# A second table that fixes the place of some 290 of the first 430 instructions

## The chip, the cores and the metric

The kernel runs on one core of one Trainium2 chip. The metric is the device time of one execution in microseconds (us). The kernel before took 1061.97 us, the median of three runs (1061.06, 1062.64 and 1061.97).

## What is computed

Three layers follow each other, all in float32 with an accuracy that plain single-pass matmuls would not give:

```
attention:  q, k, v of shape (4, 12, 448, 64): batch, heads, tokens, width of a head
            q, k are divided by their root mean square and multiplied by g_q, g_k
            softmax(q k^T / 8) v
layer 1:    x (1792 x 768) @ w_in (768 x 1024) -> h;  h * softmax(h), layer norm times g_ln,
            @ w_out (1024 x 768)
layer 2:    x (1792 x 768) @ w_in (768 x 2048) -> h;  h - tanh(h), @ w_out (2048 x 768)
```

The weights arrive as 64-bit floats and are turned into pairs of 32-bit halves (a high part and the rest) on the chip.

## The kernel before

Attention works on 24 pairs of heads. For each pair p: `load_qk` and `load_v` fetch the data; `norm` squares, sums and scales (tiles sq, ss, nr, rr, qn; on VectorE for the first two pairs, on GpSimd for the others); `qk_trans` transposes on TensorE (qkps) and splits the result into high and low parts (wk, wq), and eight DMAs spread these over the tiles k and q, of which there are three each, used in turn; `maxima` multiplies q by k once in a rough form (mps) and takes the row maximum on VectorE (nm); `spread` transposes the maxima (nmps, nt) and a DMA puts them as an extra row into q; `weights` makes the exact scores (sps), and ScalarE takes their exponential (pf); `pv` multiplies by v (pvps); `pv_fin` and `x_norm` divide and write the result to xd. Tiles mps and sps share three PSUM buffers, pvps has two, and qkps, nmps and the others share three.

Pair 0 is made in another way than the rest: its scores come from four matmuls with a contraction over 64 rows each (rows 0 to 63 for the first head, 64 to 127 for the second), while every later pair has two matmuls over 128 rows. In the profile these are `sps<-q,k 64*128` and `sps<-q,k 128*128`. The transposes (112 rows), pair 1's mps (128 rows) and most of pvps (128 rows) use the whole height of the array.

None of this is issued in the order in which it is written. A recorder takes down some 4,000 operations, `place` plays them through a list scheduler with estimated costs (`cost`) and a table of offsets by tile name (`SHIFT`), and `give` issues them in the order found, on all engines' queues at once. Where the planner expects TensorE to wait, `fill` puts dummy matmuls in front of the instruction that is waited for: 128x128 products of a tile of ones (`idle<-still`), whose number is the expected wait divided by a fixed cost. Each is two passes in the profile. Their number is settled in `place`:

```
n = int((start - since - 0.1) / took)
...
for _ in range(n):
    ...
    order.append(op)
```

Every operation is recorded from one line, L206, so the rows of the profile tell operations apart by their tiles. Each engine executes its own queue strictly in the order issued; SyncE's queue holds nearly all DMA issues. A DMA takes one of eight semaphores in turn, and its issue waits until the one eight places ahead of it has landed. The recorded stretch holds the attention and the beginning of layer 1; the first 430 operations of it are what the change touches.

Of the kernel before, what the change touches and what calls it, by code (L numbers as in the profile page):

```python
# [167 lines left out]
def _real(x):  # L168
# [14 lines left out]
    "wq scalar": -28, "wq vector": -149, "x scalar": -868, "x2d sync": 478, "x2ps tensor": 274, "xd sync": -164,  # L183
    "xo scalar": -435, "xo vector": -40, "xr sync": 224, "xs scalar": -251, "xs vector": 13, "xu scalar": -29,
    "xu vector": -999, "zero vector": 166,
}


class Recorder:
# [307 lines left out]
    slack, doubt = (0.12, 0.39), 0.97  # L497
    still = None

    def give(self):  # L500
        order = self.plan()
        self.on = False
        with self.tc.manual_schedule():
            for op in order:
                self.take(op.queue, op.what, op.f, op.a, op.kw)
        self.ops = []
# [884 lines left out]
```

## Time and profile before

| | us |
|---|---|
| median of three runs | 1061.97 |
| profiled execution, its own time | 1057.57 |
| span of the profiled execution | 1055.5 |
| TensorE busy in the span | 1037.0 (98%) |
| VectorE busy | 686.8 (65%) |
| ScalarE busy | 490.9 (47%) |
| GpSimd busy | 234.8 (22%) |
| granted TensorE clock, mean | 1.00 of full |

The profile is of one execution. Its time is the span and 2.07 us around it. "Busy" TensorE contains the dummy matmuls, and the ends of matmuls are modelled, so the 98% does not mean that useful products fill the span. In the tables by stretch, a row gives for each engine the busy time in the stretch and the count of instructions, then the granted clock, the mean busy share of the 16 DMA engines and what they moved.

### The profile page before, as it was taken

The numbers are of one execution on the slowest core, as the hardware profiler recorded it, in microseconds if no ns is written. First come the engines' busy times: TensorE is split into PE (matmuls) and PEld (weight loads), VectorE is DVE, ScalarE is ACT, GpSimd is POOL, SyncE is SP. The second block draws the span as 40 slices with busy tenths as digits, with TensorE's granted clock in tenths as the row PEclk, the third lists the DMA queues.
The fourth block names the chain that finished last, engine by engine and source line by source line (L and its number), as shares of the span: only waits on it lengthen the run. The fifth ranks groups of instructions, "written<-read, shape, count | busy, mean of one in ns | idle before, by whom it ended". The sixth has DMA issues, their size and how long they took to land.

```text
span 1055.5 us, 15572 instructions
## 1 busy us (share of the span) xinstructions
PE 1037.0 (98%) x5550; PEld 877.5 (83%) x5550; DVE 686.8 (65%) x1312; ACT 490.9 (47%) x996; POOL 234.8 (22%) x204
## 2 busy tenths in 40 slices
PE   9999999999998999999999999999999999999998
PEld 7665686768866788787999999898989999998988
DVE  8877867988898533538731373666768576765434
ACT  5878867898887543742451443212222221212110
POOL 3423132221203100025000251413333241412000
PEclk9999999999999999999999999999999999999999
DMA  7899988998999994676865421212212021110004
GB/s 190 237 243 228 253 256 251 257 250 274 288 301 253 307 291 159 202 251 200 289 215 189 165 71 51 60 60 60 61 40 79 22 61 42 59 60 1 1 30 179
DMA packets 112469, 171.20 MB, mean 162 GB/s; under 512 B 30656, under 2 KB 78216, under 8 KB 112392
## 3 DMA queue, kind: packets, MB, share of 16 engines
q1 hardware_dynamic: 112368, 170.20, 55.0%
q8 instruction: 44, 0.72, 0.3%
q14 instruction: 33, 0.27, 0.1%
q10 hardware_dynamic: 24, 0.01, 0.0%
HBM read 109.32 MB, written 29.10 MB: 131 GB/s over the span
## 4 chain that ended last, share of the span: by engine, by line
PE 81%; DMA 7%; DVE 5%; ACT 3%; issue 1%; SPq 1%; POOL 1%; DVEq 0%; ACTq 0%; POOLq 0%
PE ops L206 22%; PE h2ps L206 22%; PE x2ps L206 9%; PE hps L206 9%; PE pvps L206 8%; PE sps L206 5%; PE mps L206 3%; DMA q<-wq 2%; DMA xr<-xd 1%; DVE val L206 1%; PE qkps L206 1%; DMA q<-nt 1%; SPq L206 1%; DMA raw<-in_moe_w_in_dram 1%; PE idle L206 1%
## 5 line engine op out<-in xcount | busy, mean ns | idle before, releaser
L206 PE MATMUL ops<-w,gT 128*128 128x384 f32 x1344 | 257.5, 336 | 0.0
L206 PE MATMUL h2ps<-x2s,w 128*128 128x512 f32 (+1 forms) x1152 | 256.4, 365 | 0.0
L206 PEld LDWEIGHTS ops<-w,gT 128*128 128x128 f32 x1344 | 235.8, 188 | 8.4
L206 PEld LDWEIGHTS h2ps<-x2s,w 128*128 128x128 f32 x1152 | 200.2, 188 | 27.8
L206 DVE SCALAR_TENSOR_TENSOR val<-raw,val 128x512 int32<-128x512 int32 (+1 forms) x192 | 147.4, 771 | 58.9 <-POOL val L206 56.7
L206 DVE TENSOR_TENSOR ob<-ops,ob 128x384 f32<-128x384 f32 x196 | 108.4, 554 | 102.4 <-PE ops L206 102.0
L206 POOL TENSOR_TENSOR w<-val,w 128x512 fp32r<-128x512 f32 x60 | 80.8, 1348 | 374.0 <-ACT w L206 363.3
L206 PE MATMUL pvps<-pf,va 128*128 128x448 f32 (+1 forms) x384 | 156.5, 555 | 0.0
L206 DVE TENSOR_REDUCE nm<-mps 128x1 f32<-128x448 f32 x168 | 100.0, 618 | 53.0 <-PE mps L206 52.5
L206 PE MATMUL hps<-w,xs 128*128 128x256 f32 (+1 forms) x828 | 126.2, 308 | 2.3 <-ACT hb L206 2.3
L206 PE MATMUL sps<-q,k 128*128 128x448 f32 (+2 forms) x400 | 125.8, 431 | 2.8 <-DMA q<-nt 1.6
L206 PEld LDWEIGHTS hps<-w,xs 128*128 128x128 f32 x828 | 114.5, 190 | 12.0 <-ACT hb L206 3.2
L206 PE MATMUL x2ps<-lnT,w 128*128 128x384 f32 (+1 forms) x720 | 121.4, 326 | 0.3 <-DVE lnT L206 0.3
L206 PEld LDWEIGHTS x2ps<-lnT,w 128*128 128x128 f32 x720 | 116.8, 188 | 3.4 <-issue 2.2
L206 ACT ACTIVATE th<-h2ps 128x512 f32<-128x512 f32 (+1 forms) x64 | 34.8, 544 | 179.3 <-PE h2ps L206 167.0
L206 PEld LDWEIGHTS sps<-q,k 128*128 128x128 f32 (+2 forms) x400 | 67.4, 182 | 44.2 <-issue 22.1
L206 ACT ACTIVATE pf<-sps 128x448 f32<-128x448 f32 (+1 forms) x169 | 87.0, 537 | 21.6 <-PE sps L206 20.3
L206 PEld LDWEIGHTS pvps<-pf,va 128*128 128x128 f32 (+1 forms) x384 | 60.2, 188 | 36.8 <-issue 33.2
L206 POOL TENSOR_SCALAR val<-raw 128x512 f32<-128x512 f32 x48 | 77.8, 1622 | 32.7 <-DMA raw<-in_moe_w_out_dram 13.2
L206 ACT ACTIVATE gT<-th 128x512 fp32r<-128x512 f32 (+1 forms) x64 | 37.1, 579 | 99.4 <-PE ops L206 66.8
L206 POOL TENSOR_TENSOR qn<-qk,rr 112x512 f32<-112x512 f32 x44 | 50.4, 1165 | 114.7 <-issue 30.9
L206 DVE TENSOR_TENSOR th<-h2ps,th 128x512 f32<-128x512 f32 (+1 forms) x64 | 39.8, 621 | 43.8 <-ACT th L206 43.7
(95 smaller groups left out, 990.2 us busy)
## 6 DMA issues: line engine op xcount, KB each, us to landing
w<-w_out SPq DMA_DIRECT2D x48, 512.0 KB
raw<-in_moe_w_in_dram SPq DMA_DIRECT2D x36, 512.0 KB
raw<-in_moe_w_out_dram SPq DMA_DIRECT2D x36, 512.0 KB
w<-w_in SPq DMA_DIRECT2D x24, 512.0 KB
k<-wk SPq DMA_DIRECT2D x46, 224.0 KB
q<-wq SPq DMA_DIRECT2D x46, 224.0 KB
w_in<-w SPq DMA_DIRECT2D x12, 512.0 KB
w_out<-w SPq DMA_DIRECT2D x12, 512.0 KB
```

The lines of the kernel that those rows point to most:

```text
L206: return f(*[_real(x) for x in a], **{n: _real(x) for n, x in kw.items()})
```

## The change

A table `PLACE` maps the number of an operation (the sequence in which it was recorded) to a position. `placed` first cuts the planned order into groups: an operation with the dummy matmuls that stand ahead of it. Groups named in the table go to the positions given there; the others fill the positions that are left, in their planned sequence. The table has 287 entries with positions up to 428; from position 429 on nothing is moved. The planner itself, its costs and the number of dummy matmuls are as before: the dummies travel with the instruction that they stand ahead of.

```diff
+PLACE = {
+    3: 0, 4: 3, 266: 4, 157: 5, 158: 6, 81: 7, 7: 9, 83: 10, 6: 11, 82: 12, 261: 13, 160: 14, 0: 15, 79: 16, 8: 19,
...
+}
...
+    def placed(self, order):
+        still, groups = [], []
+        for op in order:
+            still.append(op)
+            if op.at >= 0:
+                groups.append(still)
+                still = []
+        rest = iter([g for g in groups if g[-1].at not in PLACE])
+        held = {PLACE[g[-1].at]: g for g in groups if g[-1].at in PLACE}
+        return [op for n in range(len(groups)) for op in (held[n] if n in held else next(rest))] + still
+
     def give(self):
-        order = self.plan()
+        order = self.placed(self.plan())
```

Three places show what moves. In these rows k_182 and q_167 are pair 0's k and q before, k_156 and q_164 the same tiles after; k_163 and q_177 (before), k_161 and q_166 (after) belong to pair 1.

GpSimd's first instructions, before:

```order
L1372 MEMSET const-uint8-127 128x1
L1386 UNCONDITIONAL_BRANCH
masks.py:197 MEMSET idf 128x128
L206 MEMSET va 128x7x64 x2
masks.py:199 ISA
masks.py:199 AFFINE_SELECT idf<-idf 128x128
L206 CAST q_167<-zero 64x448 x2
L206 CAST q_177<-zero 64x448 x2
L206 CAST q_185<-zero 64x448 x2
```

And after:

```order
L1412 MEMSET const-uint8-127 128x1
L1426 UNCONDITIONAL_BRANCH
masks.py:197 MEMSET idf 128x128
masks.py:199 ISA
masks.py:199 AFFINE_SELECT idf<-idf 128x128
L235 CAST q_164<-zero 64x448
L235 CAST q_166<-zero 64x448
L235 CAST q_164<-zero 64x448
L235 CAST q_166<-zero 64x448
L235 MEMSET va 128x7x64
```

Two memsets of v's tiles leave the place ahead of the identity matrix idf and come far later.

TensorE around the longest row of dummies, before:

```order
L206 MATMUL mps<-k_182,q_167 128x448
L206 MATMUL nmps<-idf,nm 4x128
L206 MATMUL mps<-wk,qd_155 128x448
L206 MATMUL idle<-still 128x128 x4
L206 MATMUL nmps<-idf,nm 4x128
L206 MATMUL idle<-still 128x128 x18
L206 MATMUL mps<-k_163,q_177 128x448
L206 MATMUL sps<-q_167,k_182 128x448 x3
L206 MATMUL sps<-q_167,k_163 128x448
L206 MATMUL sps<-q_167,k_182 128x448 x3
```

And after:

```order
L235 MATMUL mps<-k_156,q_164 128x448
L235 MATMUL sps<-q_164,k_156 128x448
L235 MATMUL idle<-still 128x128 x4
L235 MATMUL nmps<-idf,nm 4x128
L235 MATMUL sps<-q_164,k_156 128x448 x2
L235 MATMUL nmps<-idf,nm 4x128
L235 MATMUL sps<-q_164,k_156 128x448
L235 MATMUL mps<-wk,qd_150 128x448
L235 MATMUL idle<-still 128x128 x18
L235 MATMUL mps<-k_161,q_166 128x448
L235 MATMUL sps<-q_164,k_161 128x448
L235 MATMUL sps<-q_164,k_156 128x448
```

Five sps matmuls of pair 0 have come ahead of the 18 dummies, which are as many as before: three of them, with one nmps and one mps, between the nmps that waits for the last maximum and the dummies, one ahead of that nmps, and one further ahead (not shown).

TensorE behind the dummies, where the rest of pair 0's scores is made, before:

```order
L206 MATMUL mps<-k_163,q_177 128x448
L206 MATMUL sps<-q_167,k_163 128x448
L206 MATMUL qkps<-idf,qn 128x112
L206 MATMUL mps<-k_163,q_177 128x448
L206 MATMUL qkps<-idf,qn 128x112 x7
L206 MATMUL sps<-q_167,k_182 128x448
L206 MATMUL mps<-k_163,q_177 128x448
L206 MATMUL sps<-q_167,k_182 128x448 x2
L206 MATMUL nmps<-idf,nm 4x128
L206 MATMUL sps<-q_167,k_163 128x448
L206 MATMUL sps<-q_167,k_182 128x448 x3
L206 MATMUL sps<-q_167,k_163 128x448
```

And after:

```order
L235 MATMUL sps<-q_164,k_161 128x448
L235 MATMUL qkps<-idf,qn 128x112
L235 MATMUL sps<-q_164,k_156 128x448
L235 MATMUL qkps<-idf,qn 128x112
L235 MATMUL mps<-k_161,q_166 128x448
L235 MATMUL qkps<-idf,qn 128x112
L235 MATMUL sps<-q_164,k_156 128x448
L235 MATMUL qkps<-idf,qn 128x112
L235 MATMUL sps<-q_164,k_156 128x448 x2
L235 MATMUL mps<-k_161,q_166 128x448
L235 MATMUL sps<-q_164,k_161 128x448
L235 MATMUL mps<-k_161,q_166 128x448
```

Transposes, rough scores and exact scores now alternate one by one. Counted from pair 1's first mps to the first pvps, pair 0's sps stood in 5 unbroken runs before and stand in 12 after. Further on, the two pvps matmuls over 64 rows, which stood side by side, are separated by others.

## Rows read from the trace of the kernel before

**Rows 1.** The page: busy time, share of the span, instructions of each engine.

```profile
PE 1037.0 (98%) x5550; PEld 877.5 (83%) x5550; DVE 686.8 (65%) x1312; ACT 490.9 (47%) x996; POOL 234.8 (22%) x204
```

**Rows 2.** Busy time by stretch: start:end, length, engines, clock, DMA share, GB/s.

```profile
0.00:25.00 25.00, 22.62 (x152) 19.81 (x153) 21.49 (x61) 13.38 (x33) 8.04 (x17) 1.00 0.83 199
25.00:55.00 30.00, 29.58 (x141) 19.50 (x141) 25.17 (x53) 23.73 (x54) 12.39 (x12) 1.00 0.87 228
...
350.00:400.00 50.00, 49.30 (x291) 41.37 (x291) 19.20 (x31) 23.45 (x53) 0.84 (x3) 1.00 1.00 302
```

**Rows 3.** The same view for the dummies alone (PE, PEld, clock, DMA).

```profile
0.00:25.00 25.00, 17.65 (x122) 16.47 (x122) 1.00 0.83 199
25.00:55.00 30.00, 2.20 (x14) 2.18 (x14) 1.00 0.87 228
```

**Rows 4.** Chain that ended last, first 60 us: start, length, what.

```profile
0.86 0.89 POOL va L206 x2
...
21.67 2.81 DMA q<-wq
```

**Rows 5.** TensorE's timeline 18 to 29 us: start, length, instructions [idle before].

```profile
19.87 0.27 PE L206 MATMUL nmps<-idf,nm 128*4 128x128 f32 x1
19.98 4.18 PE L206 MATMUL idle<-still 128*128 128x128 f32 x36
24.47 0.44 PE L206 MATMUL mps<-k,q 128*128 128x448 f32 x1 [0.31 <-DMA q<-wq]
24.85 3.41 PE L206 MATMUL sps<-q,k 64*128 64x448 f32 x19
28.19 0.47 PE L206 MATMUL mps<-k,q 128*128 128x448 f32 x1
28.59 0.47 PE L206 MATMUL sps<-q,k 64*128 64x448 f32 x1
28.99 0.32 PE L206 MATMUL qkps<-idf,qn 112*128 112x112 f32 x1
```

**Rows 6.** The same timeline, 29 to 34 us.

```profile
29.45 0.83 PE L206 MATMUL qkps<-idf,qn 112*128 112x112 f32 x7
30.21 0.47 PE L206 MATMUL sps<-q,k 64*128 64x448 f32 x1
30.61 0.47 PE L206 MATMUL mps<-k,q 128*128 128x448 f32 x1
31.01 0.67 PE L206 MATMUL sps<-q,k 64*128 64x448 f32 x2
...
31.81 1.34 PE L206 MATMUL sps<-q,k 64*128 64x448 f32 x9
33.08 0.47 PE L206 MATMUL mps<-k,q 128*128 128x448 f32 x1
33.88 0.47 PE L206 MATMUL mps<-k,q 128*128 128x448 f32 x1 [0.33 <-ACT pf L206]
```

**Rows 7.** The same timeline, 36 to 47 us.

```profile
36.33 1.67 PE L206 MATMUL pvps<-pf,va 128*128 128x448 f32 x4
37.83 0.55 PE L206 MATMUL qkps<-idf,qn 112*128 112x112 f32 x4
38.31 1.02 PE L206 MATMUL pvps<-pf,va 64*128 64x448 f32 x4
39.27 1.49 PE L206 MATMUL sps<-q,k 128*128 128x448 f32 x6
...
45.62 0.38 PE L206 MATMUL idle<-still 128*128 128x128 f32 x2
46.09 1.09 PE L206 MATMUL sps<-q,k 128*128 128x448 f32 x4
```

**Rows 8.** TensorE's waits, 55 to 500 us: total, times, longest. The costliest.

```profile
PE mps L206 <- ACT pf L206: 3.4, 4, 1.5
```

**Rows 9.** VectorE's timeline: the last row maximum ahead of the 18 dummies.

```profile
18.77 0.62 DVE L206 TENSOR_REDUCE nm<-mps 128x1 f32<-128x448 f32 x1 [0.57 <-PE mps L206]
```

24 rows, old and new, of the table PLACE are left out of this document.

## The prediction

> **What bounds the kernel now.** I read the page first, then the tables by stretch, the chain, and TensorE's timeline around the change. TensorE is busy for 98% of the span [rows 1], at a granted clock of 1.00 in every stretch [rows 2], so the other engines, at 65% and less, can only matter through waits that they cause. But the first stretch is not what it seems: of the 22.6 us that TensorE is busy in the first 25 us, 17.65 are dummies [rows 2, 3]. From 25 to 55 us the dummies are 2.20 of 29.58 [rows 2, 3]. So there are two regimes under the 430 instructions: up to about 24.5 us TensorE waits for the first two pairs to come through loads, norms and DMAs; from then on its own products set the pace. Behind 55 us its costliest wait sums to 3.4 us up to 500 us [rows 8]. A delay of TensorE's queue at the point where the order is the old one again therefore goes through to the end, apart from what such waits swallow.
>
> The seam is the first mps of pair 1. It starts at 24.47, after 36 dummy passes from 19.98 to 24.16, and has waited 0.31 us for the DMA that brings wq into q [rows 5]; the chain names the same DMA, 2.81 us from 21.67 [rows 4].
>
> **Ahead of the seam.** Three things move. First, GpSimd's two memsets, 0.89 us on the chain [rows 4], leave the place ahead of the identity matrix. VectorE's casts can start that much sooner, but behind them its queue now has the k-side and q-side steps in another order, and ScalarE takes a weight conversion ahead of q's copy and another ahead of wq's. I cost this at nothing, because everything in it ends at the last row maximum of pair 0 (18.77 to 19.39, [rows 9]), which is one reduction in a queue with as many as before. If the cover is gone, the gain is the 0.9 us, the loss about as much.
>
> Second, five sps come ahead of the seam. The nmps that waits for that last maximum starts at 19.87, and 0.11 later the 18 dummies begin [rows 5]. Now three sps, one nmps and one mps stand between: three times 0.20, 0.10 and 0.20, and some 0.5 for going back and forth between the 64-row and the full-height form (priced below): 1.4 us. The dummies, unchanged in number, are issued behind them. Before they take from 19.98 to 24.16, of which the end of the last pass overlaps what follows, so some 4.0 us at issue [rows 5], so the seam comes at 19.87 + 0.11 + 1.4 + 4.0 = 25.4 instead of 24.47. That is 0.95 later, while the DMA has long landed. Third, in return five sps are done, 5 x 0.20 = 1.0 us. The sum ahead of the seam is nothing. In words: the gap was filled with dummies already, so useful work put into it pushes the dummies instead of replacing them. Bounds: -1.9 if the start is 0.9 earlier as well, +0.9 if it is that much later.
>
> **Behind the seam.** Here the change pays, since pair 0's scores are cut from 5 runs into 12. A 64-row sps in a long run costs little: 19 of them take 3.34 us, from 24.85 to 28.19, 0.18 each [rows 5]. Alternating with others it is dear: a full-height mps and one sps take 0.80 together, from 28.19 to 28.99 [rows 5], and again from 30.21 to 31.01 [rows 6]; at 0.20 each that is 0.40 too much for one run. Beside transposes it is less: seven of them from 29.45, at 0.10 apiece, end at about 30.15 and the sps behind them starts at 30.21 [rows 6], so only the way back costs. I take 0.35 for a run. Of the seven runs more, I count five on the path: at two places TensorE would have to wait anyway, for an exponential of ScalarE that frees a PSUM buffer and for a maximum. Five times 0.35 is 1.75; the ends are 0 (all of it lies in such waits) and 2.8 (seven at 0.40).
>
> The Trainium skill, "TensorEngine Tiling (Array Packing)", section "Key Properties", says that changing the tiling mode drains TensorE, while changing the tile within a mode does not. By that rule every one of the 14 changes of form more would cost the same 0.20 that an mps shows, 2.8 us; the trace agrees beside mps, and disagrees where a transpose goes ahead of an sps. With the rule's sum in place of mine the forecast would be about 1 us later.
>
> Two more losses. Nine sps from 31.81 are through by the next mps at 33.08 [rows 6]: 1.27 us where nine times 0.20 would be 1.80, since the two heads' matmuls in different halves of the array overlap there. These nine now stand in five runs: +0.5 (from 0 to 0.9). And the two pvps over 64 rows, four passes from 38.31 to 39.27, take 0.96 together, against 1.50 for four passes of the full height from 36.33 to 37.83 [rows 7]; apart, each half has the array to itself: +0.5 (0 to 0.54).
>
> On the other side stand the waits that the mixing can remove. Between the mps at 33.08 and that at 33.88 there is 0.80 instead of 0.20, for ScalarE's pf [rows 6], and two dummy passes end their issue at about 45.84 while the sps behind starts at 46.09 [rows 7]. Together 0.85; I take 0.6 as gone (0 to 0.85).
>
> **The sum.** 0 + 1.75 + 0.5 + 0.5 - 0.6 = 2.15 us at the end of the moved stretch. SyncE's queue is moved too: two loads of v go ahead of the last half of pair 1's q, two raw weight loads go sooner. Both lie under the dummies, so I cost them at nothing; if the cover were gone, the two loads of v would cost the time of two issues ahead of pair 1's second head. Of the 2.15 I let 0.9 through, 1.9 us. The profiled execution would go from 1057.57 to 1059.5; it lies 4.4 below the median, and I move the median by the same amount, to 1063.9. About 0.2%, or 2.1 us, is what a measurement of this kernel can tell from no change.
>
> **The rivals.**
> - Rival 1, the mixing works: not slower. Its place is the seam and the 8 us behind it. The start is 0.9 earlier, so the dummies end at 24.5 as before, and the five sps count in full, -1.0. The waits go, -0.85, and the switches and the lost overlap hide in the waits for exponentials, since ScalarE is busy for 23.7 of the 30 us from 25 to 55 [rows 2]. -1.85 gives 1060.1. It decides for this if the seam is at 24.6 or sooner. For it: the memsets were on the chain. Against it: in the runs shown the price of 0.40 stood between neighbours that waited for nothing.
> - Rival 2, clearly slower. All seven runs are on the path, 2.8, with 0.9 and 0.54 of overlap lost, no wait removed, and the sps ahead of the seam are bought at par: 4.2 us, 1066.2. From 2.1 us at the end of the moved stretch on the change can be told from none.
> - Rival 3, the shift is swallowed. The DMA engines are fully busy from 350 to 400 us (1.00, [rows 2]); if the transfers and not TensorE's queue set the pace there, a late start costs nothing: 1062.0.
>
> **How the numbers follow.** Forecast 0.38, rival 1 0.33, rival 2 0.18, rival 3 0.11. Faster by over 0.2%: about half of rival 1, whose own doubt of 1.5 us reaches beyond -2.1, and a little of rival 3: 0.18. Slower: rival 2 and nearly half of the forecast: 0.36. The same: the rest, 0.46. The range goes from 1059.2, which leaves out a third of rival 1, to 1066.8, just above rival 2; the forecast's own range is 1062.4 to 1065.5.
>
> **What would show it.** In the profile after, the 36 dummy passes should start near 21.4 and pair 1's first mps near 25.4, with no wait for a DMA. From there to the first pvps (35.45 before) TensorE's timeline should show single sps with 0.40 to the next instruction, and the first pvps should start two to three us later than before. The two 64-row pvps should take over 0.7 us each. Wrong would be a seam at or ahead of 24.5, sps between transposes at 0.20 each, or TensorE waiting for pf at many places behind the seam.

## The result, and the profile after

The changed kernel takes 1074.05 us (median of 4 runs, 1073.60 to 1075.77) against 1062.31 for the kernel before (4 runs, 1061.06 to 1063.78): a ratio of 1.0113, with a 95% interval of 1.0095 to 1.0131. The forecast was 1063.9 with a range to 1066.8. It was wrong, by 10 us and on the slow side. The profiled execution of the changed kernel spans 1073.9 us.

The busy share of the page hides it: TensorE is at 98% as before [rows 1], but for 14.7 us more.

```profile
PE 1051.7 (98%) x5550; PEld 882.9 (82%) x5550; DVE 689.1 (64%) x1312; ACT 492.0 (46%) x996; POOL 235.4 (22%) x204
```

The table by stretch shows it. It has the same stretches as [rows 2] (start:end, length, busy time and instructions of PE, PEld, DVE, ACT and POOL, granted clock, DMA share, GB/s), and below them two stretches cut where the clock changes.

```profile
0.00:25.00 25.00, 22.39 (x146) 19.06 (x147) 21.25 (x59) 12.63 (x31) 6.02 (x15) 1.00 0.70 185
25.00:55.00 30.00, 29.95 (x95) 16.34 (x94) 17.91 (x37) 14.61 (x32) 11.43 (x11) 0.72 0.60 152
350.00:400.00 50.00, 49.81 (x249) 39.96 (x250) 33.55 (x75) 30.42 (x61) 9.06 (x10) 0.97 1.00 308
...
29.00:32.70 3.70, 3.70 (x15) 1.89 (x13) 1.86 (x4) 2.72 (x7) 2.97 (x3) 1.00 0.89 284
32.72:49.78 17.06, 17.01 (x39) 8.75 (x39) 10.91 (x21) 6.27 (x15) 4.57 (x5) 0.50 0.60 141
```

From 25 to 55 us TensorE is busy for 29.95 of 30 us and gets through 95 instructions where it had 141 in 29.58 us. The granted clock is 0.72 there, which is 0.50 (1.2 GHz) from 32.72 to 49.78 us and 1.00 (2.4 GHz) on both sides. Before, it was 1.00 throughout. Ahead of the fall TensorE did not idle: 3.70 of 3.70 us busy from 29.0 to 32.7, but with 15 instructions. The same cut of the kernel before has 22, also with 3.70 busy:

```profile
29.00:32.70 3.70, 3.70 (x22) 2.61 (x23) 2.53 (x5) 2.75 (x7) 2.27 (x3) 1.00 0.81 263
```

TensorE's timeline after, around the seam (start, length, instructions, idle before and its releaser). It answers to [rows 5, 6]:

```profile
20.34 0.27 PE L235 MATMUL nmps<-idf,nm 128*4 128x128 f32 x1
20.55 0.68 PE L235 MATMUL sps<-q,k 64*128 64x448 f32 x2
21.16 0.27 PE L235 MATMUL nmps<-idf,nm 128*4 128x128 f32 x1
21.36 0.47 PE L235 MATMUL sps<-q,k 64*128 64x448 f32 x1
21.76 0.47 PE L235 MATMUL mps<-wk,qd 128*128 128x448 f32 x1
22.07 4.18 PE L235 MATMUL idle<-still 128*128 128x128 f32 x36
26.00 0.45 PE L235 MATMUL mps<-k,q 128*128 128x448 f32 x1
...
29.88 0.47 PE L235 MATMUL sps<-q,k 64*128 64x448 f32 x1
30.28 0.32 PE L235 MATMUL qkps<-idf,qn 112*128 112x112 f32 x1
30.52 0.47 PE L235 MATMUL sps<-q,k 64*128 64x448 f32 x1
30.93 0.31 PE L235 MATMUL qkps<-idf,qn 112*128 112x112 f32 x1
...
32.74 0.74 PE L235 MATMUL mps<-k,q 128*128 128x448 f32 x1
33.41 0.74 PE L235 MATMUL sps<-q,k 64*128 64x448 f32 x1
34.19 0.74 PE L235 MATMUL mps<-k,q 128*128 128x448 f32 x1
...
43.85 5.44 PE L235 MATMUL pvps<-pf,va 128*128 128x448 f32 x6
48.41 2.18 PE L235 MATMUL sps<-q,k 128*128 128x448 f32 x5
50.42 3.18 PE L235 MATMUL pvps<-pf,va 128*128 128x448 f32 x7
...
57.92 0.45 PE L235 MATMUL mps<-k,q 128*128 128x448 f32 x1
60.47 0.71 PE L235 MATMUL idle<-still 128*128 128x128 f32 x4 [2.10 <-ACT nt L235]
```

Read it from the top. The seam is at 26.00 without a wait. Then single 64-row sps and single transposes alternate, 0.40 and 0.24 apart. At 32.74, behind the fall of the clock, a form of mps that took 0.45 takes 0.74. The last line is a wait that the kernel before doesn't have: dummies need the PSUM buffer that ScalarE empties with nt, and ScalarE now does four other things ahead of it:

```profile
58.81 0.54 ACT L235 ACTIVATE pf<-sps 128x448 f32<-128x448 f32 x1
59.38 0.31 ACT L235 ACTIVATE nr<-ss,eps 112x16 f32<-112x16 f32 x1
59.59 0.56 ACT L235 ACTIVATE xo<-xo 128x448 f32<-128x448 f32 x1
60.06 0.20 ACT L235 ACTIVATE rr<-nr 112x16 f32<-112x16 f32 x1
60.16 0.25 ACT L235 ACTIVATE nt<-nmps 4x128 fp32r<-4x128 f32 x1
```

To compare the runs I take four marks from the timelines: the first gps; pair 1's first mps (the seam); the first pvps; and the qkps that starts at 60.17 us of the kernel before, behind the moved part, from where on all orders are the same. "Stretch" below is the time from the first mark to the last, "at 0.50" the time at that clock up to the last mark.

| kernel | gps | seam | first pvps | qkps | stretch | at 0.50 | ratio to before, 95% |
|---|---|---|---|---|---|---|---|
| before | 6.85 | 24.47 | 35.45 | 60.17 | 53.32 | 0 | 1 |
| changed | 8.07 | 26.00 | 43.85 | 74.81 | 66.74 | 17.07 | 1.0113 (1.0095, 1.0131) |
| e1 TensorE alone | 6.84 | 34.22 | 53.14 | 89.03 | 82.18 | 37.5 | 1.0262 (1.0229, 1.0296) |
| e2 the others alone | 8.46 | 25.14 | 38.29 | 69.17 | 60.71 | 3.41 | 1.0078 (1.0048, 1.0107) |
| e3 changed, dummies | 8.42 | 27.55 | 43.28 | 71.43 | 63.01 | 3.41 | 1.0078 (1.0049, 1.0107) |
| e4 up to the seam | 7.99 | 25.93 | 36.37 | 61.31 | 53.33 | 0 | 1.0004 (0.9984, 1.0025) |
| e5 changed, regrouped | 8.40 | 27.52 | 42.88 | 75.72 | 67.32 | 20.5 | 1.0118 (1.0093, 1.0143) |
| e6 before, alternating | 6.85 | 24.37 | 43.20 | 69.32 | 62.47 | 13.65 | 1.0095 (1.0071, 1.0119) |
| e7 = e3, nt earlier | 8.38 | 26.32 | 42.05 | 68.90 | 60.52 | 0 | 1.0060 (1.0036, 1.0084) |
| e8 = e3, one row | 8.32 | 26.25 | 52.00 | 84.97 | 76.64 | 30.7 | 1.0198 (1.0160, 1.0236) |
| e9 = e6, dummies | 6.85 | 23.93 | 43.61 | 69.15 | 62.30 | 6.83 | 1.0101 (1.0084, 1.0119) |
| e10 before, dummies | 7.21 | 24.60 | 37.73 | 62.47 | 55.26 | 0 | 0.9999 (0.9988, 1.0010) |
| e11 before up to here | 6.84 | 23.92 | 34.87 | 59.60 | 52.75 | 0 | 0.9997 (0.9985, 1.0009) |
| e12 = e5, dummies | 7.62 | 25.54 | 41.59 | 74.26 | 66.63 | 10.24 | 1.0119 (1.0099, 1.0138) |

The stretch of e11, which up to the last mark is the kernel before, is 0.57 us shorter than that of the kernel before: so much can two executions differ, and smaller differences in this column say nothing.

The whole difference between the two profiled executions up to 170 us is there at the last mark: +14.64 us at the qkps (1.22 of it at the first gps, 13.42 in the stretch), +13.99 at an hps at 169.88. The two short falls of the clock behind it (3.41 us each, at 128.3 and 350.2) are of a kind that executions of the kernel before have too: its mean granted clock was 0.996 and 0.997 in two series of 20 and 23 runs, though its profiled execution has none. That execution, 1057.57 us, is at the fast end of its kernel and that of the changed one, 1075.77, at the slow end, so the medians differ by 11.7 and not by 18.

### The profile page after: what moved, and what is told of

The parts are those of the page before. It is cut to its first block, busy times and chain, and to the rows that moved or that the text cites. A ratio compares the mean times of both kernels' runs of the same rounds, so it can differ in the third digit from the quotient of the medians.

```text
span 1073.9 us, 15567 instructions
## 1 busy us (share of the span) xinstructions
PE 1051.7 (98%) x5550; PEld 882.9 (82%) x5550; DVE 689.1 (64%) x1312; ACT 492.0 (46%) x996; POOL 235.4 (22%) x204
## 4 chain that ended last, share of the span: by engine, by line
PE 85%; DMA 7%; DVE 3%; ACT 3%; issue 1%; SPq 1%; POOL 0%; ACTq 0%; DVEq 0%; POOLq 0%
PE ops L235 22%; PE h2ps L235 22%; PE pvps L235 10%; PE x2ps L235 10%; PE hps L235 9%; PE sps L235 5%; PE mps L235 3%; PE qkps L235 1%; PE idle L235 1%; DMA q<-wq 1%; DMA xr<-xd 1%; DMA xd<-xo 1%; DVE val L235 1%; SPq L235 1%; PE lps L235 1%
## 5 line engine op out<-in xcount | busy, mean ns | idle before, releaser
L235 PE MATMUL pvps<-pf,va 128*128 128x448 f32 (+1 forms) x384 | 162.6, 569 | 0.0
L235 PE MATMUL sps<-q,k 128*128 128x448 f32 (+3 forms) x400 | 133.3, 443 | 1.0 <-DMA q<-nt 0.5
L235 PEld LDWEIGHTS sps<-q,k 128*128 128x128 f32 (+3 forms) x400 | 69.2, 185 | 44.5 <-issue 25.1
```

The costliest lines, as they stand in the source:

```text
L235: return f(*[_real(x) for x in a], **{n: _real(x) for n, x in kw.items()})
```

## The experiments

Two theories stood at the start. The clock theory: TensorE's new sequence behind the seam lets the granted clock fall, and that is most of the cost. The rival "the others": the new order of ScalarE, VectorE and SyncE keeps TensorE waiting. Orders were changed by the table alone, so a diff shows the first lines that differ, with the cuts marked. The diffs of e1 to e5 and e7 are against the changed kernel, that of e8 is against e3, and those of e6 and e11 are against the kernel before.

**e1: TensorE's queue as changed, the others as before.** Some 25 instructions of the others had to follow their operands.

```diff
 PLACE = {
-    3: 0, 4: 3, 266: 4, 157: 5, 158: 6, 81: 7, 7: 9, 83: 10, 6: 11, 82: 12, 261: 13, 160: 14, 0: 15, 79: 16, 8: 19,
...
+    14: 77, 15: 78, 73: 97, 53: 98, 96: 99, 74: 145, 75: 146, 117: 147, 129: 148, 118: 149, 130: 150, 138: 154,
...
```

> TensorE's 163 instructions of the moved stretch stand in the changed order; the other engines keep the order of the kernel before, but for some 25 instructions that their operands force to move. Clock theory (TensorE's own new order lets the granted clock fall, and that is most of the cost): a stretch at 0.50 again begins near 33 us and lasts some 10 to 17 us, 1068 to 1074 us. Rival 'the others' (the new order of ScalarE, VectorE and SyncE starves TensorE, and its clock falls because it waits): clock 1.00, first pvps near 36 us, 1061 to 1064 us. Rival of the prediction on record (switches, late seam and lost overlap alone): clock 1.00 and 1063 to 1065 us.

Measured: 1091.68 us, far outside what any theory gave. The clock fell three times up to the last mark. The fall at 17.68 us is ahead of the seam, 0.19 us behind a wait of 1.48 us for a maximum, and the one at 72.30 us begins 1.1 us behind a wait of 2.26 us for pf. Only the one at 41.58 us is what the clock theory said: in the alternation, with TensorE busy throughout ahead of it (first row below). The waits come on top (3.3 us for maxima, 2.3 for pf). A sequence that is half of a changed plan costs more than the whole.

```profile
37.80:41.50 3.70, 3.70 (x14) 1.96 (x13) 0.70 (x2) 2.62 (x5) 3.70 (x4) 1.00 0.45 148
...
17.70:31.30 13.60, 12.06 (x42) 8.84 (x42) 7.65 (x16) 3.49 (x9) 2.26 (x2) 0.50 0.48 115
41.60:62.00 20.40, 18.94 (x43) 10.08 (x43) 9.24 (x20) 5.79 (x13) 3.85 (x5) 0.50 0.51 123
```

**e2: the others as changed, TensorE's queue as before.**

```diff
 PLACE = {
...
-    35: 47, 12: 48, 54: 49, 13: 50, 41: 55, 55: 56, 62: 57, 59: 61, 57: 67, 64: 70, 42: 71, 43: 72, 66: 74, 67: 75,
...
+    35: 47, 12: 48, 54: 49, 13: 50, 55: 52, 59: 57, 57: 59, 60: 60, 61: 61, 14: 63, 38: 64, 39: 65, 40: 66, 41: 67,
...
```

> TensorE keeps the order of the kernel before; VectorE, ScalarE, GpSimd and SyncE stand in the changed order. Clock theory: clock 1.00 from 5.4 us to the last stage, pair 1's first mps between 24.5 and 26 us, 1061 to 1065 us. Rival 'the others': TensorE waits in the stretch of 30 to 60 us as in the changed kernel, 1068 to 1074 us, with or without a stretch at 0.50.

Measured: 1070.17 us, the rival's number. The clock fell for 3.41 us, at 35.00, where the clock theory had it at 1.00. TensorE's costliest waits from 24 to 72 us (total, times, longest):

```profile
PE mps L231 <- DVE nm L231: 2.9, 3, 1.6
PE mps L231 <- ACT pf L231: 1.1, 2, 0.8
PE sps L231 <- ACT pf L231: 0.5, 1, 0.5
```

So the others' new order does cost waits where TensorE keeps the old one: with the smaller ones 5.1 us, of the 7.39 by which the stretch is longer. But in the changed kernel, where both are new, these waits are not there; of its waits in the same stretch only nt (2.1) and one for pf (0.6) are listed. e1 and e2 together show that the halves don't add up (+29.9 and +8.4 for a whole of +11.7), and cannot by themselves say which half is to blame.

**e3: the changed kernel with 10 dummies where it alternates.** They write where the next instruction writes anyway.

```diff
+HOLD = {192: 1, 193: 1, 166: 1, 161: 1, 194: 1, 195: 1, 173: 2, 181: 2}
...
             for op in order:
+                for _ in range(HOLD.get(op.at, 0)):
+                    n = min(128, op.out.shape[1])
+                    self.tensor.matmul(
+                        op.out[:, :n], lhsT=self.still, rhs=self.still[:, :n], start=True, stop=True
+                    )
                 self.take(op.queue, op.what, op.f, op.a, op.kw)
```

> The changed kernel with 10 more dummy matmuls (20 instructions of 0.11 us, 2.2 us of TensorE) between the single sps, transposes and mps just behind the seam, into PSUM that the next instruction writes anyway. Clock theory: the granted clock stays 1.00 through 25 to 50 us; about half of the 17.07 us at 0.50 comes back, 8.5 us, less 2.2 us of dummies: 1074 - 8.5 + 2.2 = 1067.7, between 1065.5 and 1070 us. Rival 'the others' and the rival that the clock falls for a reason outside this stretch: the stretch at 0.50 stays, and the time is 1074 to 1077 us. Were the clock to cost nothing because other work ends last there, the clock would be 1.00 and the time still 1073 to 1077 us.

Measured: 1070.72 us, just above the clock theory's range: work was added and the kernel became faster (a ratio to before of 1.0078 against 1.0113, each against its own runs of before; the ends of the intervals overlap by 0.0012, so the gain is barely clear of noise). The clock held behind the seam:

```profile
29.00:32.70 3.70, 3.70 (x22) 2.41 (x21) 2.21 (x7) 2.42 (x5) 1.42 (x2) 1.00 0.88 254
...
32.50:50.00 17.50, 17.18 (x74) 9.94 (x73) 12.66 (x24) 10.34 (x24) 7.09 (x8) 1.00 0.71 180
```

The profiled execution lost 3.41 us at 0.50 elsewhere, from 8.81 us, under the first dummies. That is why its seam is at 27.55.

**e4: the changed order up to the seam, the old one behind it.**

```diff
 PLACE = {
...
-    113: 150, 853: 151, 76: 152, 854: 155, 216: 158, 218: 159, 855: 160, 135: 164, 217: 165, 219: 167, 145: 170,
...
+    113: 150, 853: 151, 76: 152, 854: 155, 216: 158, 218: 159, 855: 160, 153: 162, 159: 163,
...
 }
```

> The changed order on all engines up to pair 1's first mps and nothing behind it: 99 positions, POOL's memsets and the five sps ahead of the seam included. Clock theory: clock 1.00, pair 1's first mps at 25.4 to 26 us, 1061 to 1064 us. Rival 'the start' (the slower start, with gps at 8.07 us where it was at 6.85 us, is a cost of its own): 1064 to 1067 us with the clock at 1.00. If the fall of the clock were set up by what stands ahead of the seam, a stretch at 0.50 shows here too, and over 1068 us.

Measured: 1061.82 us, as the clock theory said. The stretch takes 53.33 against 53.32 us. Its seam is at 25.93 and the five sps ahead of it are done, as the prediction's sum of nothing had it. The stretch is counted from the first gps, and that comes 1.14 us later than before; the medians show no cost of this, but their interval reaches 2 us to either side.

**e5: the changed kernel, TensorE's 52 instructions between seam and first pvps in their old sequence.**

```diff
-    163: 171, 152: 176, 164: 182, 165: 183, 178: 184, 128: 185, 192: 187, 189: 188, 116: 189, 115: 190, 870: 191,
...
+    152: 175, 128: 182, 116: 184, 115: 185, 870: 186, 857: 187, 153: 188, 858: 189, 179: 190, 864: 191, 220: 192,
...
```

> The changed kernel, with TensorE's 52 instructions between pair 1's first mps and the first pvps back in the sequence that they have among themselves in the kernel before (pair 0's 64-row sps in long runs again); all else as changed but for three instructions of VectorE and ScalarE that must follow. Clock theory (single 64-row sps between transposes let the clock fall): clock 1.00 from 25 to 60 us, pair 0's 32 sps cost 6.0 to 7.3 us in all (10.46 in the changed kernel), what stays is the later seam and the waits behind, 3 to 5 us: 1064 to 1068 us. Rival 'the others' (the clock falls because the other engines' order keeps TensorE short of work): a stretch at 0.50 stays, over 1070 us.

Measured: 1073.85 us, the rival's side. Behind the seam the clock held to 36.02 and then fell for 13.65 us; waits for nm (0.9 in two), nt (2.1) and pf (0.8) are there. Ahead of the fall TensorE was not busy throughout:

```profile
32.32:36.02 3.70, 3.41 (x16) 2.04 (x15) 2.52 (x5) 2.70 (x8) 3.64 (x5) 1.00 0.87 276
```

Long runs alone don't keep the clock, under an order of the other engines that was made for another sequence. This undid my expectation that the alternation is the one condition. Nor is the clock all of this kernel's loss: one of its four runs had a mean clock of 0.997, as the kernel before has, and took 1071.36 us.

**e6: the kernel before, with only that sequence changed.** Five instructions of VectorE, ScalarE and GpSimd had to follow. Its table:

```diff
+PLACE = {
+    131: 164, 132: 165, 133: 166, 134: 167, 148: 185, 149: 186, 150: 187, 151: 188, 175: 189, 176: 190, 152: 191,
+    177: 192, 186: 193, 187: 194, 178: 198, 188: 199, 179: 200, 189: 202, 190: 203, 867: 205, 223: 206, 226: 207,
...
+    232: 255, 225: 256, 244: 257, 233: 258, 268: 259, 234: 260,
+}
```

> The kernel before, with TensorE's instructions between pair 1's first mps and the first pvps, and no others, in the sequence of the changed kernel (five instructions of VectorE, ScalarE and GpSimd have to follow). Clock theory: the granted clock falls to 0.50 between 29 and 37 us, and the time is 1067 to 1074 us. Rival of the prediction on record (the alternation costs only its switches and lost overlap): clock 1.00, pair 0's 32 sps at 8 to 9.5 us in all where they took 6.0, 1063 to 1066 us. Rival 'the others': no loss, 1061 to 1063 us.

Measured: 1071.48 us. The clock theory's condition came (a fall at 32.20 us, for 13.65) and so did its time. One new wait came with it, 1.2 us of the nmps for wk. The two cuts:

```profile
28.50:32.20 3.70, 3.70 (x14) 1.88 (x14) 0.62 (x1) 2.67 (x5) 3.70 (x4) 1.00 0.72 243
...
32.00:46.00 14.00, 12.74 (x30) 6.44 (x30) 6.42 (x12) 4.84 (x12) 1.73 (x3) 0.51 0.55 134
```

The alternation is enough to let the clock fall, with the other engines' order as it was but for those five: 14 instructions in 3.70 us of full busy share, and then 0.50. The wait for wk comes behind the fall, at 35.65 us. This is the nearest thing to the whole loss in one edit: +9.15 of the changed kernel's +13.42 us in the stretch.

**e7: e3, and nt of pair 2 four instructions ahead on ScalarE.**

```diff
-    316: 354, 317: 355, 309: 356, 347: 357, 348: 358, 404: 360, 373: 365, 286: 366, 301: 367, 423: 368, 424: 369,
...
+    316: 354, 317: 355, 309: 356, 347: 357, 348: 358, 404: 359, 332: 363, 373: 364, 286: 365, 301: 366, 356: 367,
+    296: 369, 285: 370, 423: 371, 424: 372, 333: 373, 425: 375, 426: 376, 427: 377, 923: 378, 924: 379, 364: 380,
...
```

> The changed kernel with the 10 dummies of the run before that held its clock, and one more edit: on ScalarE the nt of pair 2's first nmps goes four instructions ahead, to where it waits only for its nmps. If ScalarE's new order is what makes TensorE's next dummies wait, that wait falls from 2.10 us to under 0.8 us, and all behind 60 us comes 1.2 to 2 us earlier than with the dummies alone, counted from the first gps. If the wait is of another engine's making (VectorE's nm is late), it stays at 2.1 us.

Measured: TensorE's wait for nt goes from 2.10 to 0.8 us, so ScalarE's order made it; 1067.85 us (two runs). Here the clock is 1.00 from 4 us to the last stage, which makes it the copy to measure the clock against. From the mps that starts at 32.74 in the changed kernel to the pvps at 50.42, the same instructions in the same order take 17.68 us there and 10.85 here:

```profile
34.97 0.45 PE L239 MATMUL mps<-k,q 128*128 128x448 f32 x1
...
45.82 3.56 PE L239 MATMUL pvps<-pf,va 128*128 128x448 f32 x8
```

Of the 10.85, two dummies are some 0.5, so the clock costs 6.8 to 7.3 us.

That the clock fell, or held, is not a chance of single profiles: the mean granted clock is 0.989 to 0.992 in all eight runs of the changed kernel and e6, and 0.995 to 1.000 in all eight of e3 and e7.

**e8: e3, with dummies on one row.**

```diff
-                        op.out[:, :n], lhsT=self.still, rhs=self.still[:, :n], start=True, stop=True
+                        op.out[:, :n], lhsT=self.still[:1], rhs=self.still[:1, :n], start=True, stop=True
```

> The changed kernel with the same 10 dummies at the same places, each on one row of TensorE instead of 128: equal in instructions, columns and PSUM written. If the clock goes by how long TensorE is busy or how many columns it streams, it holds at 1.00 through 25 to 50 us as with the full dummies, 1068 to 1072 us. If it goes by how much of the array works (which would also explain why 64-row sps and transposes let it fall at a busy share of 1.00), a stretch at 0.50 begins between 30 and 40 us again, 1073 to 1078 us.

Measured: 1081.76 us, and worse than either number. The clock fell at 31.55 us for 27.31 us:

```profile
32.50:50.00 17.50, 17.45 (x48) 10.50 (x49) 5.91 (x10) 5.60 (x11) 2.58 (x3) 0.50 0.42 99
```

As many dummies, of as many columns, on one row did not hold the clock that the full-height ones held in e3. One thing weakens it: beside transposes the one-row dummies bring changes of form of their own (ahead of the fall the two passes of one take 0.40 us to the next start, those of a full-height one in e7 0.31), so the spacing was another too. And a count of instructions is no rule for the fall: the stretch ahead of it has as many here as the like stretch of e7, where the clock held (e8, then e7):

```profile
27.80:31.50 3.70, 3.70 (x20) 2.36 (x20) 2.11 (x7) 2.26 (x5) 1.52 (x2) 1.00 0.82 243
...
29.00:32.70 3.70, 3.70 (x20) 2.52 (x20) 0.98 (x3) 2.29 (x5) 2.65 (x3) 1.00 0.88 282
```

**e9 and e10: e6 and the kernel before, each with the dummies of e3.** Both edits are the HOLD lines of e3.

> The kernel before with TensorE's changed sequence behind the seam alone (the run that lost its clock for 13.65 us and took 62.47 us from the first gps to the first qkps behind the moved stretch, where the kernel before takes 53.32 us), now with the 10 full dummies at the same eight instructions. Clock theory: clock 1.00 through 60 us; that stretch takes 53.3 + 2.5 of dummies + 3 of switches and lost overlap = 58.8 us, between 57.5 and 60.5, and the kernel 1064 to 1069 us. Rival (the sequence itself costs the 9 us, and the clock follows from it): 62 to 65 us for the stretch, 1070 to 1075 us.

> The kernel before with the same 10 dummies and its own order: what the dummies cost where nothing else is changed. If they lie on TensorE's path with their full length, first gps to the qkps behind the stretch takes 53.3 + 2.5 = 55.8 us and the kernel 1062 to 1065 us; if they fall into slack, 53.3 to 54.5 us and no change. The clock is 1.00 in this stretch either way.

Measured: e9 1070.87 us, with 62.30 for the stretch. Both are the rival's numbers, and the clock theory's were missed. The dummies put the fall off, to 38.26 us, and cut it from 13.65 to 6.83, but the stretch is no shorter than that of e6 (62.47). By an estimate, half of the 6.82 us less at 0.50 came back, 3.4; the dummies cost 2.54 of it and a new wait for a maximum 0.32, and the rest is within what two executions differ by. The wait for wk is as long as in e6, but here it is ahead of the fall, which begins 1.28 us after it:

```profile
36.98 0.27 PE L218 MATMUL nmps<-idf,nm 128*4 128x128 f32 x1 [1.21 <-DVE wk L218]
```

e10 takes 1060.85 us, no change; in its stretch the dummies cost 55.26 - 53.32 = 1.94 us. Of the 2.30 us by which its profiled execution is late at 60 us, 0.48 are left at a qkps at 229.62: a delay of this size is swallowed by later waits, most of it.

**e11: a version meant to beat both.** The kernel before, with dummies where TensorE waits anyway.

```diff
+KEEP = {945: (3, "ps_m", "m"), 954: (2, "ps_m", "m"), 3136: (6, "ps_m", "m"), 3226: (5, "ps_m", "m")}
...
+                if op.at in KEEP:
+                    n, pool, tag = KEEP[op.at]
+                    ref = Ref(self, self.pools[pool], [128, 128], F32, tag, "idle")
+                    for _ in range(n):
+                        self.tensor.matmul(ref, lhsT=self.still, rhs=self.still, start=True, stop=True)
```

> A version meant to beat both: the kernel before, with 16 dummies ahead of four mps at which TensorE waits for ScalarE, VectorE or a DMA (0.59 to 1.49 us, at 112, 114, 331 and 334 us), in a PSUM tile of their own. In most traces of this study the clock was 0.50 for 3.41 or 6.83 us near one of these two places, a loss of some 1.7 us each time. If the dummies hold it there, the median falls by 1 to 3 us, to 1058 to 1061 us where the kernel before stands at 1061 to 1062; if the falls come from somewhere else, or the dummies push what waits, no change or up to 1 us slower.

Measured: 1061.18 us, a ratio of 0.9997 (0.9985 to 1.0009). The mean granted clock over its 12 runs is 0.9988 against 0.9971 for 23 of before, so something was held, but no time was won. No version of this study beats the kernel before.

**e12: e5 with the dummies of e3.**

> The changed kernel with TensorE's stretch between pair 1's first mps and the first pvps back in the sequence of before (the run that still lost its clock, for 13.65 us from 36 us) and the 10 dummies on top. Clock theory: clock 1.00 through 60 us, and first gps to the qkps behind the stretch takes 53.3 + 2.5 of dummies + 2.1 of the wait for nt + up to 2 of other waits and switches = 58 to 60 us (67.32 without the dummies); 1064 to 1069 us. Rival 'the others' (the other engines' changed order costs the time, whatever the clock): 63 us or more for the stretch, over 1070 us.

Measured: 1073.12 us and 66.63 for the stretch: the rival's numbers. Here the others' order does cost TensorE directly:

```profile
36.70 0.83 PE L237 MATMUL idle<-still 128*128 128x128 f32 x6
40.05 0.47 PE L237 MATMUL mps<-wk,qd 128*128 128x448 f32 x1 [2.52 <-DVE nm L237]
```

In long runs TensorE gets to this mps before VectorE has the maximum in its changed place, and 1.25 us after the wait the clock falls (at 41.30 us, for 6.83). The changed kernel doesn't wait there.

## Why the prediction was wrong

**Where the time went.** The stretch takes 13.42 us more. The comparison with e7 gives 6.8 to 7.3 of it to the clock. nt is 2.1. What is left is 4.0 to 4.5, and e7 shows its kind at full clock (times from each start to the next start on TensorE, passes in brackets; a wait counts with the instruction ahead of it):

| | before | changed | e7 |
|---|---|---|---|
| 64-row sps (32) | 6.01 | 10.46 | 9.02 |
| full-height sps (32) | 7.60 | 10.65 | 9.78 |
| transposes qkps (42) | 4.33 | 5.85 | 5.00 |
| pvps (32) | 10.34 | 12.10 | 9.94 |
| mps (29) | 9.92 | 12.77 | 10.22 |
| planned dummies (106) | 14.33 | 13.37 | 12.77 |
| added dummies (20) | | | 2.54 |
| nmps and gps (9) | 0.80 | 1.53 | 1.24 |

Rows of neighbours must be read together: where an sps stands behind a pvps, e7 has 0.03 to the start of the sps and 0.55 from there (44.43 and 44.46 us), where inside runs it is 0.38 and 0.20. So the full-height sps of e7 did not cost 2.2 us more and its pvps did not get cheaper; the two rows together are 19.72 against 17.94.

By medians the clock's part is the same size: the mean granted clock of the changed kernel's four runs is 0.9902, of the 43 runs of before in e1 to e4 and e9 to e12 0.9966, and the difference of 0.0064 over 1070 us is 6.9 us of the 11.7.

**The step that failed** is in the sum behind the seam: "Behind the seam. Here the change pays". Each run was priced at 0.35 us of TensorE's time, at a clock taken as given because it was "1.00 in every stretch [rows 2]". The price of a run was right, but the clock was not a constant: the same alternation that costs 0.35 a run let it fall. I read "busy" as "at work". The two rows at 29 us, 3.70 us busy with 22 and with 15 instructions, are the difference. The fall alone cost 6.8 to 7.3 us, in a sum that had 2.15 for everything.

**Ahead of the seam: right but for the start.** Five sps ahead push the dummies: the 36 passes start at 22.07 (predicted near 21.4) and the seam is at 26.00 (25.4), with no wait for the DMA; e4 puts the sum at 0.01 us in the stretch. The start, which I had at nothing, is not 0.9 earlier for the memsets but 1.22 later at the first gps, and 0.55 at the first mps; at the last mark e4 is 1.14 late.

**The switches: mechanism right, size too small.** A single sps to the transpose behind it takes 0.40 and back 0.24, so a pair of one each costs 0.64 where 0.30 would be the sum: 0.34 a run, of which 0.14 is the way from a transpose to an sps, which I had read as free. Together with the lost overlap of the two heads the 64-row sps cost 3.0 us more at full clock (9.02 against 6.01, with a wait of 0.3 in it), and the transposes 0.7 more, where I had 1.75 + 0.5 within bounds of 0 and 3.7. The rule that a change of the tiling mode drains TensorE, which the prediction cites from the Trainium skill, "TensorEngine Tiling (Array Packing)", section "Key Properties", would have put the first of the two terms at 2.8, nearer to what came.

**The 64-row pvps: size too small.** Apart, each takes 0.95 to the next start in e7 (0.48 and 0.47 before, [rows 7]): +0.95 together, above the 0.54 that I had as the end. That is about half of the 1.78 us by which pvps and full-height sps together grew; some 0.3 of the rest are waits, and for the others I had no term.

**The waits: wrong sign.** I took 0.6 off for waits that go. They went (the 0.33 for pf of [rows 6] is not there), but a wait of 2.10 for nt came, from ScalarE's queue, where I had looked for order changes only at the start.

**What gets through.** I let nine tenths through, 1.9 of 2.15 us. That was too much for a small delay: of e10's 2.30 us a fifth is left (0.48), so on such a shift the third rival was nearer. The large one goes through: 14.64 at 60 us, 13.99 at 170. For the change as it is that rival is out: the changed kernel still loses with DMA shares of 1.00 from 350 to 400 us.

**The rivals.** "Mixing works" asked for a seam at 24.6 or sooner. "Clearly slower" named the right sign and the right place, 64-row runs on the path, with a price of 4.2. Without the fall of the clock the profiled stretch would be some 6 us longer (e7's 60.52, less 2.54 for the dummies, plus 1.3 for nt, less 53.32), so the forecast would have been too low even then, but within reach of that rival. The first pvps, forecast two to three us later than before, came 8.40 later (43.85).

The Trainium skill, "TensorE: Matmul & The Clock Gate", section "HAM oscillation — how this bites in real kernels", has the clock fall where TensorE sits idle between bursts, waiting for data. The trace of the changed kernel disagrees, as far as the busy share goes, in which the ends of matmuls are modelled: TensorE was busy for 3.70 of 3.70 us ahead of the fall, and so it was in e6. Waits and then a fall, which look like what that section tells, are in e12 (2.52 us), e9 (1.21) and the first fall of e1 (1.48).

**What stays open.** Why the clock of e5 fell at 36.02 us though its runs were as long as in the kernel before, whose clock held, is not settled: TensorE's waits in the ten us ahead of it are 0.24 and 0.29 us. Nor does a wait decide it alone: the wait of 2.10 us for nt is followed by a fall of 3.41 us in e5, e8 and e12 and by none in the changed kernel and e3. Which part of the alternation lets the clock fall, the half-height sps, the transposes or the gaps between the forms, was not separated, and e8 changed the rows of the dummies and their spacing at once.

## What to carry to other kernels

A busy share of 1.00 doesn't say that TensorE's clock is safe. Look also at how many instructions a stretch gets through (no rule, as e7 and e8 show, but here it was the sign), and before spreading half-height products between transposes, price the fall as a case of its own: here 17.07 us at 0.50, some 7 us, more than all switches and waits together. A few dummies of full height between them cost 2.5 us and held it in e3 and e7; in e9, where a wait followed, they only put the fall off. And an order is made for all queues at once: either half of this one, put alone against the other engines' old order, lost time, and TensorE's alone lost 2.5 times what the whole lost.

## What was not expected of the hardware

- The granted clock falls to 0.50 behind 3.70 us in which TensorE's busy share is 1.00, and it stays there: 17.07 us in the changed kernel, 13.65 in e6, 27.31 in e8.
- The kernel before has short falls in most executions: only 7 of 43 runs in those two series have a mean clock of 1.000. A single profiled execution with none, as the one the prediction was read from, shows a safer kernel than there is.
- A one-row dummy next to a transpose takes 0.40 us for its two passes at the full clock, a full-height one 0.31 (e8, e7).
